# Starting the MLP's first layer early, and replacing in place: one change to a top-k attention and mixer kernel

## The chip, the cores and the metric

The kernel runs on one core of one Trainium2 chip. The time is device microseconds of one execution; the median of seven runs of the kernel before is 1774.5 us (1771.52 to 1776.44).

## The reference

For 8 batches and 8 heads, 576 rows and 64 columns a head. Each row of scores keeps what is not below its 32nd largest value:

```
scores = scale * np.matmul(q, k.transpose(0, 1, 3, 2))
kth = np.partition(scores, -top_k, axis=-1)[..., -top_k:-top_k + 1]      # top_k = 32
scores = np.where(scores >= kth, scores, -1e9)
attn = exp(scores - max) / (sum + 1e-9);  x = attn @ v, heads side by side: (8, 576, 512)
u = x + (x.transpose(0, 2, 1) @ U @ V).transpose(0, 2, 1)                # rank 32
out = u + np.maximum(u @ w_ch1, 0.0) @ w_ch2                            # 512 -> 2048 -> 512
```

q, k and v are float32; U, V and the two weights are float64 and are turned into float32 on the chip.

## The kernel before, in words

**Steps.** A batch has four pairs of heads, a pair five row chunks (four of 128 rows for each of the two heads, and one in which both heads' last 64 rows share the partitions). So there are 8 × 4 × 5 = 160 steps n, with pair g = n // 5 and chunk t = n % 5. A step with t < 4 works on two score chunks of 128 x 576 (one per head), a step with t = 4 on one.

**One step's work.** `scores` multiplies q by k on TensorE into PSUM, and ScalarE copies the result into an Ssb tile (three buffers); it is issued one step ahead. `front` finds the 32nd largest value on VectorE in four rounds of eight: MAX8 gives the eight largest of a chunk (L385, L399), MATCH_REPLACE8 overwrites them with a very small number (L395), and so on. In the kernel before every replacement writes a new rr tile, of which there are three buffers. The two chunks of a step alternate: replacement, replacement, MAX8, MAX8. Then POOL (L402, L403, L421) and ScalarE (L420, L351) mask and exponentiate. `turns` transposes the weights E on TensorE (L474, L479), with ScalarE copying them out (L475, L480) into PT; from step 30 on one of the two heads goes through VectorE and a DRAM tile instead (`blocks`, tiles y and away), over SP's DMA queue. `values` multiplies by v (L508, L512, L498). When a pair is done, `mixed` applies the low-rank mixing and leaves u, transposed, in uT (L533 to L566).

**The MLP.** When a batch's four pairs are done, `mlp(b)` is appended to the list `fillers`. It goes over two parts of the rows (320 and 256 of the 576). In each part the first layer makes 16 hidden tiles hT of 128 x rows: four matmuls (over the four 128-wide slices `cc` of the 512 channels) into one mm tile in PSUM, which has two buffers, and one ReLU on ScalarE (L593). The second layer makes four output tiles from 16 matmuls each (L600); they are copied, u is added on POOL (L616), and a little later they are transposed back and stored by SP's queue.

**Order.** All four compute engines run what the program issues in the program's own order. The MLP's matmuls are spread between the attention's by `fill()`, called eight times a step (four times in the first 20 steps). Each call adds a fixed `share` to a budget `due` and takes matmuls from the first entry of `fillers` until the budget is used up; if there is none, `due` is set to 0. Shares are such that one MLP lasts about as long as the 20 steps of a batch; while n is at most 42 they are 0.91 of that. In the first 20 steps there is no MLP to take from. Steps 19 and 20 have a written-out order of their own, which finishes the first batch quickly.

**Weights.** `params` lists the 36 loads of U, V and slabs of the two weights; `next_params` starts one, and at later calls ScalarE (L174 to L178), VectorE (L186) and POOL (L187, L189) turn it into float32. w1 is complete before the first MLP starts.

Of the kernel before, what the change touches and what calls it, by code (L numbers as in the profile page):

```python
# [8 lines left out]
F32 = mybir.dt.float32  # L9
# [17 lines left out]
def kernel(  # L27
# [28 lines left out]
    nc = tc.nc  # L56
    B, H, S, D = q.shape
    P = 128
    C = H * D
    R = moe_U.shape[1] // 2  # L60
    F = moe_w_ch1.shape[1] // 2
# [15 lines left out]
    HT = 10  # L77
# [121 lines left out]
         [(V[:, at(t)], lambda a, t=t: a.rearrange("r (p t) -> r t p", t=NT)[:, t]) for t in range(NT)]),  # L199
        ([moe_V[:, 2 * MAIN:2 * S]] * NT, [(V[:, at(NT)], same)]),  # L200
    ]
    for f in range(0, F, SLAB):
        for cc in range(NC):
            params.append(
                ([moe_w_ch1[cc * P:(cc + 1) * P, 2 * f:2 * (f + SLAB)]], w1[:, cc, f:f + SLAB])
            )
    for c in range(0, C, P):
        for f in range(0, NF, NT):
            params.append((
# [156 lines left out]
    def front(g, t):  # L366

        if t == 0:
            dens[g] = small.tile([P, 2 * NT + 1], F32, tag="den", name="den", bufs=3)
        chunks, den = S2s.pop((g, t)), dens[g]
        n = len(chunks)
        E2 = attn.tile([P, 2 * S], F32, tag="E", name="E", bufs=3)
        Es = [E2[:, c * S : (c + 1) * S] for c in range(n)]
        sums = [den[:, 2 * t + c : 2 * t + c + 1] for c in range(n)]
        probs[g, t] = E2
        curs, ms = list(chunks), [None] * n
        first = small.tile([P, 2, 8], F32, tag="first", name="first", bufs=3)  # L380
        nmax = small.tile([P, 2], F32, tag="nmax", name="nmax", bufs=4)
        order = (1, 0) if n == 2 else (0,)
        for c in order:
            ms[c] = first[:, c]
            nc.vector.max(ms[c], curs[c])  # L385
        yield
        early, pooled, gaps = ways(g, t)
        for i in range(1, TOPK // 8):
            if i == 1:
                nc.scalar.mul(nmax[:, 0:n], first[:, 0:n, 0], -SCALE)  # L390
                for c in early:
                    weigh(chunks[c], Es[c], nmax[:, c : c + 1])
            for c in order:
                nxt = attn.tile([P, S], F32, tag="rr", name="rr", bufs=3)
                nc.vector.match_replace(nxt, ms[c], curs[c], NEG)  # L395
                curs[c] = nxt
            for c in order:
                ms[c] = small.tile([P, 8], F32, tag="m8", name="m8", bufs=8)
                nc.vector.max(ms[c], curs[c])  # L399
            yield  # L400
        for c in pooled:
            nc.gpsimd.tensor_scalar(Es[c], chunks[c], ms[c][:, 7:8], NEG, ALU.is_lt, ALU.mult)  # L402
            nc.gpsimd.tensor_tensor(chunks[c], chunks[c], Es[c], ALU.add)  # L403
        for c in early:
            nc.vector.scalar_tensor_tensor(
                out=Es[c],
                in0=chunks[c],
                scalar=ms[c][:, 7:8],
                in1=Es[c],
                op0=ALU.is_ge,  # L410
                op1=ALU.mult,
                accum_out=sums[c],
            )
        if t == NT:
            del qkTs[g]
        yield
        for c in gaps:
            least = small.tile([P, 1], F32, tag="least", name="least", bufs=3)
            nc.scalar.mul(least, ms[c][:, 7:8], WIDEN)
            nc.scalar.activation(Es[c], chunks[c], AF.Relu, bias=least, scale=-WIDEN)  # L420
            nc.gpsimd.tensor_tensor(chunks[c], chunks[c], Es[c], ALU.subtract)  # L421
            yield
        ahead = pooled if shared(g, t) else ()
        for c in ahead:
            weigh(chunks[c], Es[c], nmax[:, c : c + 1], sums[c])
            yield
        for c in order:
            if c not in early and c not in ahead:
                weigh(chunks[c], Es[c], nmax[:, c : c + 1], sums[c])
        if t == NT and g != NPAIR - 1:  # L430
            nc.scalar.activation(den, den, AF.Identity, bias=eps)
        yield
# [91 lines left out]
    def mixed(g, wait):  # L524

        b, gi = divmod(g, NPAIR)
        if gi == 0:
            uTs[b] = mlpp.tile([P, NC, S], F32, tag="uT", name="uT")
        XT, den = XTs.pop(g), dens[g]
        X = xs[g % 2]  # L530
        tp = ps_t.tile([P, NT, P], F32, tag="tp", name="tp")
        for t in range(NT):
            nc.tensor.transpose(tp[:, t, :], XT[:, cols(t)], ident)  # L533
        X4 = X[:, 0:NT, :].rearrange("p t (h d) -> p t h d", h=2)
        tp4 = tp.rearrange("p t (h d) -> p t h d", h=2)
        den4 = den[:, 0 : 2 * NT].rearrange("p (t h) -> p t h ()", h=2).to_broadcast([P, NT, 2, D])
        nc.scalar.copy(X4, tp4)
        nc.gpsimd.tensor_tensor(X4, X4, den4, ALU.mult)
        for _ in range(wait):
            yield  # L540
        pT = ps_t.tile([P, P], F32, tag="tp", name="pT")
        for t in range(NT + 1):
            i = t % NT * R
            nc.tensor.matmul(
                pT[i : i + R, :],
                lhsT=U[:, t, :],
                rhs=X[:, t, :],
                start=(t < NT),
                stop=(0 < t),
            )  # L550
        Tb = mlpp.tile([P, P], F32, tag="Tb", name="Tb")
        nc.scalar.copy(Tb, pT)
        yield
        for chunks, (lo, hi) in zip(PARTS, SPAN):
            up = ps_t.tile([P, WIDE], F32, tag="tp", name="up")
            nc.tensor.matmul(up[:, 0 : hi - lo], lhsT=Tb, rhs=V[:, lo:hi], start=True, stop=False)  # L556
            for t in chunks:
                nc.tensor.matmul(  # L558
                    up[:, OFF[t] - lo : OFF[t] - lo + rows(t)],
                    lhsT=X[:, t, :],  # L560
                    rhs=ident if t < NT else ident2,
                    is_transpose=True if t < NT else None,
                    start=False,
                    stop=(t == chunks[-1]),
                )
            nc.scalar.copy(uTs[b][:, gi, lo:hi], up[:, 0 : hi - lo])  # L566
            yield
        if gi == NPAIR - 1:
            fillers.append(mlp(b))

    def mlp(b):

        uT = uTs.pop(b)
        late = []
        for chunks, (lo, hi) in zip(PARTS, SPAN):
            w = hi - lo
            hTs = []
            for f in range(NF):
                ph = ps_m.tile([P, C], F32, tag="mm", name="mm")
                for cc in range(NC):  # L580
                    nc.tensor.matmul(  # L581
                        ph[:, 0:w],
                        lhsT=w1[:, cc, f * P : (f + 1) * P],
                        rhs=uT[:, cc, lo:hi],
                        start=(cc == 0),
                        stop=(cc == NC - 1),
                    )
                    if cc < NC - 1:
                        yield w / C
                if f % 2 == 0:  # L590
                    hT = mlpp.tile([P, 2, WIDE], F32, tag="hT", name="hT", bufs=HT)
                    hTs += [hT[:, 0], hT[:, 1]]
                nc.scalar.activation(hTs[f][:, 0:w], ph[:, 0:w], AF.Relu)  # L593
                if f == 3 and late:
                    late.pop()()
                yield w / C
            for c in range(NC):
                po = ps_m.tile([P, C], F32, tag="mm", name="mm")
                for f in range(NF):
                    nc.tensor.matmul(  # L600
                        po[:, 0:w],
                        lhsT=w2[:, f, c * P : (c + 1) * P],
                        rhs=hTs[f][:, 0:w],
                        start=(f == 0),
                        stop=(f == NF - 1),
                    )
                    if f == 9 and late:
                        late.pop()()
                    if f < NF - 1:
                        yield w / C  # L610
                oT = mlpp.tile([P, WIDE], F32, tag="oT", name="oT")
                if b == B - 1:
                    nc.vector.tensor_tensor(oT[:, 0:w], uT[:, c, lo:hi], po[:, 0:w], ALU.add)  # L613
                else:
                    nc.scalar.copy(oT[:, 0:w], po[:, 0:w])
                    nc.gpsimd.tensor_tensor(oT[:, 0:w], oT[:, 0:w], uT[:, c, lo:hi], ALU.add)  # L616
                late.append(turned_back(b, chunks, lo, c, oT))
                yield w / C
        late.pop()()
# [221 lines left out]
```

## Time and profile before

| | us |
|---|---|
| median of 7 runs | 1774.5 |
| the profiled execution, its own time | 1776.44 |
| its span, first to last instruction | 1774.7 |
| TensorE busy | 1668.6 (94%) |
| VectorE busy | 1561.4 (88%) |
| ScalarE busy | 1029.3 (58%) |
| POOL busy | 846.0 (48%) |
| MAX8, L399: 864 of 749 ns | 614.8 |
| MATCH_REPLACE8, L395: 576 of 742 ns, and 288 of 742 ns in the first round | 427.4 and 211.8 |
| first layer L581, second layer L600 | 542.6 and 547.4 |
| ReLU L593: 256 of 411 ns | 105.2 |

PE is TensorE, PEld its weight loads, DVE is VectorE, ACT ScalarE, SP the engine that issues the DMAs. A float32 matmul stands as two records in the trace. A line of the trace in order of time gives start, length, engine, source line, operation, output and inputs with shapes, how many stand together, and in brackets how long the engine was idle before and what released it. A busy share is an average over stages that have different limits, so the stages are looked at one by one.

### The profile page before, as it was taken

The page shows a single profiled execution, that of the slowest core. Times are in us where ns is not written, and L with a number is a line of the kernel's source. Part 1 is how long each engine was busy: PE and PEld are TensorE (multiplying, and loading weights), DVE is VectorE, ACT ScalarE, POOL GpSimd, SP SyncE. Part 2 cuts the span into 40 slices and gives each one's busy share as a digit, 9 for nine tenths or more (in the row PEclk, how much of TensorE's full clock was granted, in tenths as well). Part 3 has the DMA queues.
Part 4 walks back from the last instruction along what each step waited for, and adds up shares of the span by engine and source line. Part 5 has one row for each costly group of instructions (what it writes and reads, how often), then busy time and mean ns, then how long its engine had stood idle before and what let it go on. Part 6 is the DMA issues. An engine that isn't in the chain of part 4 may idle for free.

```text
span 1774.7 us, 28992 instructions
## 1 busy us (share of the span) xinstructions
PE 1668.6 (94%) x9851; PEld 1256.9 (71%) x9851; DVE 1561.4 (88%) x3106; ACT 1029.3 (58%) x2682; POOL 846.0 (48%) x591
## 2 busy tenths in 40 slices
PE   4566789999999999999999999999999999999999
PEld 2444556677777877788777877788777877788677
DVE  7999999899999999999999999999999999994000
ACT  4778777555656656565656656565656656564100
POOL 4777677535354554545445454444445444453000
PEclk7778899999999999999999999999999999999999
DMA  3222332223233232232233232232233232211010
GB/s 95 87 83 72 88 85 61 50 58 70 58 69 80 63 72 59 64 71 63 63 73 79 62 70 62 64 70 64 63 73 79 60 72 60 53 50 45 4 15 13
DMA packets 275829, 112.79 MB, mean 64 GB/s; under 512 B 173920, under 2 KB 260192, under 8 KB 275680
## 3 DMA queue, kind: packets, MB, share of 16 engines
q1 hardware_dynamic: 274624, 110.68, 26.4%
q8 instruction: 77, 1.26, 0.3%
q14 instruction: 72, 0.59, 0.1%
q10 hardware_dynamic: 1056, 0.26, 0.1%
HBM read 74.15 MB, written 36.70 MB: 62 GB/s over the span
## 4 chain that ended last, share of the span: by engine, by line
PE 76%; DVE 17%; POOL 3%; issue 2%; ACT 1%; DMA 1%; SPq 0%; POOLq 0%; DVEq 0%
PE mm L581 26%; PE mm L600 25%; DVE rr L395 8%; PE sc L333 6%; DVE m L399 6%; PE O L512 6%; PE tp L474 3%; DVE first L385 2%; PE sc L320 2%; PE O L498 2%; PE up L556 1%; PE O L508 1%; POOL E L402 1%; PE tp L648 1%; PE up L558 1%
## 5 line engine op out<-in xcount | busy, mean ns | idle before, releaser
L399 DVE MAX8 m<-rr 128x8 f32<-128x576 f32 x864 | 614.8, 749 | 5.5
L600 PE MATMUL mm<-hT,w 128*128 128x256 f32 (+1 forms) x2048 | 547.4, 410 | 0.0
L581 PE MATMUL mm<-uT,w 128*128 128x256 f32 (+1 forms) x2048 | 542.6, 411 | 3.2 <-ACT hT L593 3.2
L402 POOL TENSOR_SCALAR E<-Ssb,m 128x576 f32<-128x576 f32 x127 | 280.9, 2211 | 414.5 <-DVE m L399 412.8
L581 PEld LDWEIGHTS mm<-uT,w 128*128 128x128 f32 x2048 | 372.1, 191 | 117.5 <-issue 26.2
L600 PEld LDWEIGHTS mm<-hT,w 128*128 128x128 f32 x2048 | 368.3, 190 | 106.8 <-issue 22.5
L395 DVE MATCH_REPLACE8 rr<-m,rr 128x576 f32<-128x576 f32 x576 | 427.4, 742 | 0.0
L421 POOL TENSOR_TENSOR Ssb<-Ssb,E 128x576 f32<-128x576 f32 x159 | 225.0, 1415 | 119.6 <-ACT E L420 119.0
L351 ACT ACTIVATE E<-Ssb,nmax 128x576 f32<-128x576 f32 x288 | 223.2, 776 | 54.3 <-POOL Ssb L403 37.0
L593 ACT ACTIVATE hT<-mm 128x320 f32<-128x320 f32 (+1 forms) x256 | 105.2, 411 | 240.0 <-PE mm L581 239.6
L385 DVE MAX8 first<-Ssb 128x8 f32<-128x576 f32 x288 | 203.4, 743 | 31.5 <-ACT Ssb L346 31.5
L395 DVE MATCH_REPLACE8 rr<-first,Ssb 128x576 f32<-128x576 f32 x288 | 211.8, 742 | 0.0
L403 POOL TENSOR_TENSOR Ssb<-Ssb,E 128x576 f32<-128x576 f32 x127 | 179.1, 1410 | 10.6
L333 PE MATMUL sc<-qkT 64*128 64x288 f32 x1024 | 170.5, 454 | 6.7 <-ACT Ssb L344 5.8
L474 PE MATMUL tp<-ident,E 128*128 128x128 f32 x736 | 116.3, 284 | 36.7 <-ACT XT L521 13.9
L512 PE MATMUL O<-PT,va 128*64 128x128 f32 x2048 | 145.7, 283 | 2.0 <-DMA PT<-away 2.0
L474 PEld LDWEIGHTS tp<-ident,E 128*128 128x128 f32 x736 | 92.3, 146 | 68.6 <-ACT XT L521 15.9
L475 ACT COPY PT<-tp 128x512 f32<-128x512 f32 x184 | 106.8, 586 | 49.7 <-PE tp L474 47.2
L512 PEld LDWEIGHTS O<-PT,va 128*64 128x64 f32 x2048 | 113.5, 139 | 18.8 <-DMA PT<-away 2.7
L420 ACT ACTIVATE E<-Ssb,least 128x576 f32<-128x576 f32 x159 | 123.3, 776 | 5.2
L333 PEld LDWEIGHTS sc<-qkT 64*128 64x128 f32 x1024 | 93.1, 197 | 45.1 <-issue 14.0
L613 DVE TENSOR_TENSOR oT<-uT,mm 128x320 f32<-128x320 f32 (+1 forms) x8 | 3.6, 455 | 137.1 <-PE mm L600 137.1
(81 smaller groups left out, 1573.0 us busy)
## 6 DMA issues: line engine op xcount, KB each, us to landing
away<-y SPq DMA_DIRECT2D x416, 64.0 KB, 1.8
PT<-away SPq DMA_DIRECT2D x104, 256.0 KB, 2.8
raw<-in_moe_w_ch_dram SPq DMA_DIRECT2D x32, 512.0 KB, 3.9
va<-in_v_dram SPq DMA_DIRECT2D x64, 128.0 KB, 2.2
out_dram<-ob SPq DMA_DIRECT2D x57, 128.0 KB, 2.3
ld<-in_q_dram SPq DMA_DIRECT2D x108, 64.0 KB, 2.4
ld<-in_k_dram SPq DMA_DIRECT2D x108, 64.0 KB, 2.4
ld<-in_q_dram SPq DMA_DIRECT2D x108, 8.0 KB, 2.2
```

What stands on the lines that cost most here:

```text
L333: nc.tensor.matmul(sc[:, h, 0:HALF], lhsT=qkT[half(h), 0, cols(t)], rhs=qkT[half(h), 1, i * HALF : (i + 1) * HALF], start=True, stop=True,)
L351: nc.scalar.activation(E, chunk, AF.Exp, bias=nmax, scale=SCALE, accum_out=total)
L385: nc.vector.max(ms[c], curs[c])
L395: nc.vector.match_replace(nxt, ms[c], curs[c], NEG)
L399: nc.vector.max(ms[c], curs[c])
L402: nc.gpsimd.tensor_scalar(Es[c], chunks[c], ms[c][:, 7:8], NEG, ALU.is_lt, ALU.mult)
L403: nc.gpsimd.tensor_tensor(chunks[c], chunks[c], Es[c], ALU.add)
L421: nc.gpsimd.tensor_tensor(chunks[c], chunks[c], Es[c], ALU.subtract)
L474: nc.tensor.transpose(tp[:, j, :], E2[:, a : a + P], ident)
L512: nc.tensor.matmul(O[half(h)], lhsT=va[:, h, j, :], rhs=PB[:, j] if h and shared(g, t) else PT[:, NT * h + j], start=False, stop=(j == NT ...
L581: nc.tensor.matmul(ph[:, 0:w], lhsT=w1[:, cc, f * P : (f + 1) * P], rhs=uT[:, cc, lo:hi], start=(cc == 0), stop=(cc == NC - 1),)
L600: nc.tensor.matmul(po[:, 0:w], lhsT=w2[:, f, c * P : (c + 1) * P], rhs=hTs[f][:, 0:w], start=(f == 0), stop=(f == NF - 1),)
```

## The change

Three things change.

1. The first-layer weights w1 are loaded in another order: the slabs of the channel slices 0 and 1 first (FIRST = 2), for all of the 2048 columns, then those of the slices 2 and 3.
2. When the second pair of the first batch is mixed, a new generator `head_start` is appended to `fillers`. For the first 320 rows of batch 0 it forms, for each of the 16 hidden tiles, the sum over the two channel slices that exist by then (two matmuls), and ScalarE copies that half sum into the hidden tile's place (16 copies, eight hT buffers). When `mlp(0)` later makes these tiles, it brings the half sum back into PSUM by a matmul with the identity and adds only the slices 2 and 3: three matmuls in place of four. The second part of batch 0 and all other batches are as before.
3. In `front`, only the first round's replacement takes a new rr tile; the later rounds write the tile that they read.

```diff
+    FIRST = 2
+    for ccs in (range(FIRST), range(FIRST, NC)):
+        for f in range(0, F, SLAB):
+            for cc in ccs:
+                params.append(
+                    ([moe_w_ch1[cc * P:(cc + 1) * P, 2 * f:2 * (f + SLAB)]], w1[:, cc, f:f + SLAB])
+                )
...
-                nxt = attn.tile([P, S], F32, tag="rr", name="rr", bufs=3)
+                nxt = attn.tile([P, S], F32, tag="rr", name="rr", bufs=3) if i == 1 else curs[c]
                 nc.vector.match_replace(nxt, ms[c], curs[c], NEG)
...
+        if g == FIRST - 1:
+            fillers.append(head_start())
         if gi == NPAIR - 1:
             fillers.append(mlp(b))
+    begun = []
+    def head_start():
+        w = SPAN[0][1]
+        for f in range(NF):
+            ph = ps_m.tile([P, C], F32, tag="mm", name="mm")
+            for cc in range(FIRST):
+                nc.tensor.matmul(
+                    ph[:, 0:w],
+                    lhsT=w1[:, cc, f * P : (f + 1) * P],
+                    rhs=uTs[0][:, cc, 0:w],
+                    start=(cc == 0),
+                    stop=(cc == FIRST - 1),
+                )
+                if cc < FIRST - 1:
+                    yield w / C
+            if f % 2 == 0:
+                hT = mlpp.tile([P, 2, WIDE], F32, tag="hT", name="hT", bufs=HT)
+                begun.extend((hT[:, 0], hT[:, 1]))
+            nc.scalar.copy(begun[f][:, 0:w], ph[:, 0:w])
+            yield w / C
...
-            hTs = []
+            more = b + lo == 0
+            hTs = list(begun) if more else []
             for f in range(NF):
                 ph = ps_m.tile([P, C], F32, tag="mm", name="mm")
-                for cc in range(NC):
+                if more:
+                    nc.tensor.matmul(
+                        ph[:, 0:w], lhsT=ident, rhs=hTs[f][:, 0:w], start=True, stop=False
+                    )
+                    yield w / C
+                for cc in range(FIRST if more else 0, NC):
...
-                        start=(cc == 0),
+                        start=(cc == 0 and not more),
...
-                if f % 2 == 0:
+                if f % 2 == 0 and not more:
```

More of the change, by code (lines that the diff above doesn't have):

```diff
@@ L201 @@
     ]
-    for f in range(0, F, SLAB):
-        for cc in range(NC):
-            params.append(
-                ([moe_w_ch1[cc * P:(cc + 1) * P, 2 * f:2 * (f + SLAB)]], w1[:, cc, f:f + SLAB])
-            )
+    FIRST = 2
[5 more added lines that the diff above has]
+                )
     for c in range(0, C, P):
@@ L576, in mlp @@
             w = hi - lo
-            hTs = []
+            more = b + lo == 0
+            hTs = list(begun) if more else []
             for f in range(NF):
                 ph = ps_m.tile([P, C], F32, tag="mm", name="mm")
-                for cc in range(NC):
+                if more:
[4 more added lines that the diff above has]
+                for cc in range(FIRST if more else 0, NC):
                     nc.tensor.matmul(
```

## The prediction

> **What bounds the kernel now.** I read the page's totals and slices, then stretches of 20 us, then VectorE's, TensorE's and ScalarE's instructions in order of time, then the chain that ended last.
>
> ```profile
> span 1774.7 us, 28992 instructions
> PE 1668.6 (94%) x9851; PEld 1256.9 (71%) x9851; DVE 1561.4 (88%) x3106; ACT 1029.3 (58%) x2682; POOL 846.0 (48%) x591
> ...
> PE   4566789999999999999999999999999999999999
> ...
> DVE  7999999899999999999999999999999999994000
> ...
> PEclk7778899999999999999999999999999999999999
> ...
> PE 76%; DVE 17%; POOL 3%; issue 2%; ACT 1%; DMA 1%; SPq 0%; POOLq 0%; DVEq 0%
> ```
>
> One slice is 44.4 us. VectorE fills the first five or six, TensorE all after the eighth; the chain's 76% and 17% say the same. The stretches (PE, PEld, DVE, ACT, POOL busy) show what is free before the hand-over:
>
> ```profile
> 160.00:180.00 20.00, 8.66 (x53) 5.97 (x53) 19.86 (x42) 15.06 (x34) 15.68 (x12) 0.70 0.31 93
> 180.00:200.00 20.00, 13.18 (x94) 8.68 (x92) 19.69 (x41) 16.55 (x38) 16.42 (x12) 0.78 0.27 70
> 220.00:240.00 20.00, 15.34 (x80) 9.78 (x80) 19.86 (x41) 14.23 (x35) 14.51 (x11) 1.00 0.21 60
> ```
>
> TensorE has 7 to 11 us free in 20, but ScalarE only 3.5 to 5. From 379 us on TensorE is busy without a break but for waits of 0.4 us at 413, 2.06 at 444 and then 0.1 in each batch, so whatever moves the first matmul of the second batch's MLP (449.54 us) moves the end by as much.
>
> VectorE in order of time (a stall, then replacements of round 1 and of round 2):
>
> ```profile
> 261.39 1.42 DVE L385 MAX8 first<-Ssb 128x8 f32<-128x576 f32 x2 [3.98 <-ACT Ssb L346]
> ...
> 262.79 0.74 DVE L395 MATCH_REPLACE8 rr<-first,Ssb 128x576 f32<-128x576 f32 x1
> ...
> 263.52 0.74 DVE L395 MATCH_REPLACE8 rr<-first,Ssb 128x576 f32<-128x576 f32 x1
> ...
> 265.99 0.74 DVE L395 MATCH_REPLACE8 rr<-m,rr 128x576 f32<-128x576 f32 x1
> ...
> 266.84 0.74 DVE L395 MATCH_REPLACE8 rr<-m,rr 128x576 f32<-128x576 f32 x1
> ```
>
> Start to start the pair takes 0.73 us in round 1 and 0.85 in rounds 2 and 3. With three rr buffers the second replacement writes the buffer that the first one still reads, and waits for its end; in round 1 the source is Ssb and there is no such wait.
>
> TensorE at the end of the first batch's MLP:
>
> ```profile
> 444.48 0.56 PE L648 MATMUL tp<-ident,oT 128*128 128x128 f32 x2 [2.06 <-POOL oT L616]
> ...
> 449.54 2.69 PE L581 MATMUL mm<-uT,w 128*128 128x320 f32 x9
> ```
>
> **What the Trainium skill says.** VectorE: DVE Perf Modes, section "The DRAIN you can't avoid", has a semaphore after each of eight copies cost nothing extra. This trace differs: the wait on the instruction just in front costs 0.12 us. The next section, "Two Vector instructions with no wait between them", has an instruction that is not held start before the one in front is done; round 1 agrees (0.73 pitch under 0.74 duration). TensorE: Matmul & The Clock Gate, Part 1, has the array throttled until activity releases it; the granted clock (0.70 and 0.78 above, 1.00 from 200 us) agrees. Perfetto Trace Analysis, "Matmuls", wants groups to rotate through banks so that the emptying of one overlaps the next; here two mm tiles do, and where ScalarE was held up TensorE stood 3.22 us before L581 (239.52 us).
>
> **The change part by part.** *Replacements in place.* Rounds 2 and 3 write their own source, and the second replacement waits only for its maxima. The MAX8 behind them now waits for the first replacement, which has another instruction between: nothing, as in round 1, which has this shape. Saving 2 × 0.12 = 0.24 us in each of the 128 steps with two chunks, 31 us of VectorE in all, but worth time only where VectorE leads: 16 such steps up to step 18 (3.8 us), about two each near 261–282 and 316–337, four in 368–410, two in 418–438. Bounds per step: 0 (the gap is something else) and 0.3.
>
> *Head start.* In the order of the changed program 32 matmuls of 320 columns stand between steps 12 and 21, two of them just ahead of the scores of step 21. One costs 6.63 us / 12 = 0.55 at full clock (at most 0.79, the slowest L581 of this trace). So 17.6 to 25 us of TensorE enter a stage with 31 us free (120 to 200 us), and 16 copies of 128x320 at 0.43 (the uT copy of that size) = 6.9 us enter ScalarE, which has 3.5 to 5 in 20. Cover up to step 18: the score copies end 8 us before VectorE wants them (178.65 against 186.98). At steps 20 and 21 that slack is 1.9 and 2.8 us (203.7 against 205.62, 213.35 against 216.11). ScalarE last waits for VectorE at 165.73 (2.79 us, before L419); the 13 pair steps until then bring that point to 162.6. From there to the same instruction of step 18 (198.27) it has nine copies more, 3.9 us, and some 0.5 us of waits for their matmuls: −3.1 + 3.9 + 0.5 is about 1 us late. The two matmuls ahead of step 21's scores add 1.1 and their copy 0.4, so that the MLP starts 2.5 us later than at 214.16. VectorE's 3.8 us are then used up by waiting; behind it ScalarE's raw passes feed POOL, and scores of steps 23 and 25 follow POOL's sums (the stall shown at 261). I take +2 us at 261; bounds −3.8 (all hidden: quicker matmuls at a released clock, ScalarE's waits swallowing the copies) and +5.
>
> *First layer of part one.* 64 matmuls become 16 with the identity and 32: 16 fewer, −8.8 us. ReLUs come after three matmuls, not four: five more copies (2.2 us) before 262, five fewer after; counted in the +2. The budget `share` per fill stays, so the steps stay as full and the MLP runs out earlier by 16 × 320 columns = 20 matmuls of 256 (8.9 us at 0.44, from L600's 18 records in 3.99 us). From the second MLP's start both orders are the same.
>
> *What moves with it.* The first oT comes a step earlier: POOL's wait of 1.94 us for it at 296.5, which is on the chain, goes, and the ob copies leave ScalarE's queue ahead of the 316 stall (0.5). On SP's queue the out stores no longer stand between the four away stores at 357: 1.1 us. The last oT's wait (2.06) moves into the slack below. The reordered w1 loads keep number and size; of the changed program's 12 needed slabs the last is joined by step 10.
>
> Sum for VectorE's clock: +2 − 0.5 − 1.9 − 0.5 − 0.5 − 1.1 − 1.0 − 0.5 = −4.0 us at 438. Then TensorE, without filler for about 1.4 steps, catches up. How far: L512 of that step needs the PT transfer, fetched at 441.04 and, like the 2.97 us of the one at 360.77, landed at 444; it ran at 446.68, so 2.7 us are to be had, and up to 5 on the steps whose PT is early. I take 2.5; the rest of the 8.9 is idle. Total −6.5 us: 1776.4 becomes 1769.9 in the profiled execution (its span is 1.7 less), 1768.0 on the median of 1774.5. Behind it nothing gives it back: TensorE's step is 10.0 us (200 a batch), VectorE's drops from 9.7 to 9.5.
>
> **The rivals.**
> (a) All hidden: the copies fit into ScalarE's waits, VectorE keeps −3.8 at 261, and the total is −12 us: 1762. For it: TensorE's free 30 us and a clock that more work releases. Against: slacks of 1.9 and 2.8 us, and ScalarE above 80% busy.
> (b) It does only half: the pitch stays 0.85, or TensorE's freed 8.9 us are wholly idle because turns and values wait for E and PT: −2 us, 1772.5, within the noise. For it: VectorE is 97% busy in that stretch. Against: TensorE is 100% busy there, and round 1 has the wait-free shape.
> (c) Slower: ScalarE stands in order behind TensorE's head start at the hand-over. If each of those nine copies waits 1 us for matmuls that stand behind transposes, which wait for ScalarE themselves, and one more stall of two full mm tiles like the 3.22 us at 239 comes with it, 12 us are added: +14 at 261 in place of +2, total +5.5, 1780. It decides once the score copies of steps 20 to 25 are more than 8.5 us later than now. For it: a hand-over with 1.9 us of slack. Against: TensorE's queue there is mostly waiting, so a group is done before ScalarE asks for it.
>
> **How the numbers follow.** My forecast (1764.5 to 1771) 0.47, (a) 0.23, (b) 0.18, (c) 0.12. A measurement of this kernel tells 0.2%, 3.5 us, from no change. Faster: forecast and (a), and a quarter of (b), 0.74; same: the rest of (b) and some of (c), 0.16; slower 0.10. The range 1760 to 1776 leaves out (c) and the far end of (a); the likeliest case alone is 1764.5 to 1771.
>
> **What would show it.** Right: replacement pitch 0.73 in every round; the L581-like matmuls of the head start between 140 and 212 us with granted clock above 0.78; score copies of step 20 a little late; the second MLP's first matmul near 443 instead of 449.5, after a stretch where TensorE idles some 5 us; from there a trace shifted as a whole. Wrong: a pitch still 0.85, VectorE stalls of more than 8 us in 200–262, or TensorE with new breaks after 450.

## The result, and the profile after

The changed kernel takes 1770.5 us (median of 15 runs, 1768.7 to 1772.7) against 1775.5 us (35 runs beside it): a ratio of 0.9974, 95% interval 0.9967 to 0.9981. The gain of 5.0 us, or 4.6 by the ratio, lies within the range and on the side that was forecast; 6.5 us had been forecast. The profiled executions differ by 6.6 us in span (1774.7 and 1768.1).

The page of the changed kernel, its totals, the slices of the granted clock, and the chain:

```profile
span 1768.1 us, 29071 instructions
...
PE 1673.2 (95%) x9883; PEld 1259.3 (71%) x9883; DVE 1539.7 (87%) x3106; ACT 1032.5 (58%) x2698; POOL 846.8 (48%) x591
...
PEclk7788999998999999999999999999999999999999
...
PE 80%; DVE 10%; ACT 4%; POOL 3%; issue 2%; DMA 1%; SPq 0%; POOLq 0%; DVEq 0%
```

VectorE's busy time fell by 21.7 us with the same 3106 instructions of the same mean lengths: they stand closer together and overlap more. Its share of the chain fell from 17% to 10%, and ScalarE's rose from 1% to 4%. In the tenth slice (400 to 444 us) TensorE's clock shows an 8 that the kernel before had not.

Three of the stretches shown of before, and one more at the end of the first batch's MLP (columns: window, length, busy time and records of PE, PEld, DVE, ACT, POOL; then granted clock, DMA share, GB/s):

```profile
160.00:180.00 20.00, 13.95 (x79) 9.62 (x78) 20.00 (x44) 17.25 (x41) 15.90 (x12) 0.83 0.37 119
180.00:200.00 20.00, 17.43 (x109) 11.67 (x108) 19.61 (x41) 16.75 (x42) 13.59 (x11) 0.92 0.25 68
220.00:240.00 20.00, 17.07 (x86) 10.74 (x85) 18.48 (x38) 15.80 (x38) 15.71 (x11) 1.00 0.25 67
420.00:440.00 20.00, 14.56 (x80) 10.75 (x80) 20.00 (x42) 11.91 (x32) 11.68 (x8) 0.81 0.27 63
```

The head start fills TensorE and ScalarE before 200 us, and at 420 to 440 TensorE, which was busy for all of the 20 us before, now idles for 5.4 of them. VectorE there is busy for all of the 20.

VectorE in order of time, the same step as was shown of before:

```profile
260.21 1.42 DVE L388 MAX8 first<-Ssb 128x8 f32<-128x576 f32 x2 [3.98 <-ACT Ssb L349]
...
261.61 0.74 DVE L399 MATCH_REPLACE8 rr<-first,Ssb 128x576 f32<-128x576 f32 x1
...
262.34 0.74 DVE L399 MATCH_REPLACE8 rr<-first,Ssb 128x576 f32<-128x576 f32 x1
...
265.14 0.74 DVE L399 MATCH_REPLACE8 rr<-m,rr 128x576 f32<-128x576 f32 x1
265.80 0.07 DVE L399 MATCH_VALUE_LOAD rr<-m,rr 128x8 f32 x1
265.87 0.74 DVE L399 MATCH_REPLACE8 rr<-m,rr 128x576 f32<-128x576 f32 x1
```

The pair of round 2 now stands 0.73 us apart, as the pair of round 1 does; it was 0.85. Between the two stands a short instruction that loads the values to be looked for (MATCH_VALUE_LOAD). It now starts 0.08 us before the replacement in front ends; before, it started 0.03 us after that end (266.76, behind 265.99 + 0.74). The stall in front of the step is as long as before to the hundredth (3.98).

TensorE in order of time around the start of the second batch's MLP:

```profile
423.81 0.44 PE L684 MATMUL tp<-ident,oT 128*128 128x128 f32 x2 [1.26 <-POOL oT L652]
...
438.54 0.49 PE L512 MATMUL O<-PT,vd 128*128 128x128 f32 x2 [2.00 <-ACT uT L570]
...
440.59 2.26 PE L336 MATMUL sc<-qkT 64*128 64x288 f32 x8
442.78 4.57 PE L617 MATMUL mm<-uT,w 128*128 128x320 f32 x16
```

The second MLP starts at 442.78 instead of 449.54 us: 6.8 us, about as much as the whole result (6.6 by the spans). What follows is nearly the old trace, shifted: the fourth MLP starts 7.9 us early (843.12 instead of 850.97), and the last transfer takes 1.4 us of that back (below).

### The profile page after: what moved, and what is told of

Its sections match the earlier page's. It is cut to its first block, busy times and chain, and to the rows that moved or that the text cites. A ratio compares the mean times of both kernels' runs of the same rounds, so it can differ in the third digit from the quotient of the medians.

```text
span 1768.1 us, 29071 instructions
## 1 busy us (share of the span) xinstructions
PE 1673.2 (95%) x9883; PEld 1259.3 (71%) x9883; DVE 1539.7 (87%) x3106; ACT 1032.5 (58%) x2698; POOL 846.8 (48%) x591
## 4 chain that ended last, share of the span: by engine, by line
PE 80%; DVE 10%; ACT 4%; POOL 3%; issue 2%; DMA 1%; SPq 0%; POOLq 0%; DVEq 0%
PE mm L636 26%; PE mm L617 26%; PE sc L336 7%; PE O L516 6%; DVE rr L399 4%; DVE m L403 4%; PE tp L478 3%; PE O L502 2%; PE sc L323 2%; PE up L560 1%; DVE first L388 1%; PE O L512 1%; PE tp L537 1%; POOL E L406 1%; PE up L562 1%
## 5 line engine op out<-in xcount | busy, mean ns | idle before, releaser
L617 PE MATMUL mm<-uT,w 128*128 128x256 f32 (+1 forms) x1984 | 523.0, 409 | 0.3 <-ACT hT L629 0.3
L617 PEld LDWEIGHTS mm<-uT,w 128*128 128x128 f32 x1984 | 359.6, 190 | 110.0 <-issue 25.2
```

Source lines behind the costliest of these rows:

```text
L617: nc.tensor.matmul(ph[:, 0:w], lhsT=w1[:, cc, f * P : (f + 1) * P], rhs=uT[:, cc, lo:hi], start=(cc == 0 and not more), stop=(cc == NC - 1),)
```

## The experiments

The prediction rested on two separate things: replacements in place make VectorE faster, and the head start costs something at the hand-over and gives it back later through fewer matmuls. The sum came out about right. Whether its terms did, a time of the whole kernel can't tell; each run below does one of them alone.

**The two halves apart.** The kernel before with only the replacement changed:

```diff
-                nxt = attn.tile([P, S], F32, tag="rr", name="rr", bufs=3)
+                nxt = attn.tile([P, S], F32, tag="rr", name="rr", bufs=3) if i == 1 else curs[c]
```

> The kernel before with the replacements in place alone. Theory (both parts are needed: in place makes VectorE early up to step 19, the head start takes the matmuls that would give it back): the pitch of two replacements is 0.73 us in all rounds; VectorE reaches step 19 about 3.6 us early as in the changed kernel; the first MLP starts 2 to 3 us early, since no copies of half sums stand in ScalarE's queue; the second MLP starts 2 to 4 us early, and the time falls by 2 to 4 us (1771.5 to 1773.5). Rival A, all of the gain is the replacements': 4 to 6 us less. Rival B, all of it is the head start's: within 1 us of the kernel before.

And the changed kernel with only that line put back:

```diff
-                nxt = attn.tile([P, S], F32, tag="rr", name="rr", bufs=3) if i == 1 else curs[c]
+                nxt = attn.tile([P, S], F32, tag="rr", name="rr", bufs=3)
```

> The changed kernel with three rr tiles as before, so only the head start and the order of the w1 loads. Theory: pitch 0.85 us; VectorE on the old clock to step 19; the first MLP starts 1.5 to 3.5 us later than before; after it 16 matmuls fewer; the second MLP starts 1 to 3 us early and the time falls by 1 to 3 us (1772.5 to 1774.5). Rival A (all is the replacements'): within 1 us of before, or slower. Rival B (all is the head start's): 4 to 6 us less.

Measured: in place alone 1765.8 us, ratio 0.9949 (0.9935 to 0.9962), 9.5 us less than before; head start alone 1776.9 us, 1.0011 (1.0002 to 1.0019), 1.6 us more. In place alone is better than both kernels, and by more than the theory (2 to 4 us) or rival A (4 to 6) had expected; the head start alone came out as rival A had it. The head start takes 4.7 us from in place alone (1770.5 against 1765.8), by the medians three times what it costs without it.

VectorE in the run with in place alone, the two large stalls in front of steps 25 and 30:

```profile
258.53 1.42 DVE L385 MAX8 first<-Ssb 128x8 f32<-128x576 f32 x2 [3.98 <-ACT Ssb L346]
...
313.04 1.42 DVE L385 MAX8 first<-Ssb 128x8 f32<-128x576 f32 x2 [5.43 <-ACT Ssb L346]
```

Before, the first of them was 3.98 us as well (261.39 us, shown in the prediction), and the second 5.42:

```profile
316.44 1.42 DVE L385 MAX8 first<-Ssb 128x8 f32<-128x576 f32 x2 [5.42 <-ACT Ssb L346]
```

So a step that starts earlier doesn't wait longer for its scores. In the kernel before, the chain behind the stall at 261.39 goes back over ScalarE, POOL and TensorE to maxima of VectorE at 226.12 us, so it moves along with VectorE; only what VectorE gains between those maxima and the stall is swallowed.

The trace of in place alone is 8.93 us early at step 47 and 9.87 at the last one. That looks like 38 steps with two chunks at 0.24 us each (9.1), but it isn't: step by step the gain is uneven. Up to the start of step 19 it is 2.26 us, where 16 steps should give 3.8. In 7 of these 16 (steps 3, 6, 8, 11, 13, 16, 18) L186, VectorE's part of turning the weights into float32, becomes longer by what the replacements save. Step 3 before, and with in place alone:

```profile
46.36 1.10 DVE L186 TENSOR_SCALAR w<-w 128x512 uint32<-128x512 uint32 x1
```

```profile
45.61 1.37 DVE L186 TENSOR_SCALAR w<-w 128x512 uint32<-128x512 uint32 x1
```

Undisturbed it takes 0.41. In all seven steps of both traces it ends 0.28 or 0.29 us after an instruction of POOL ends, so it seems to be held by POOL, which in these steps moves forward by less than VectorE; no run tests this. From step 19 to step 30 another 1.1 us comes, and from step 30 on every step with two chunks pays 0.25 (14 of them up to step 47, 3.5 us). The remaining 2 us are two waits that became shorter: 0.9 at step 35, and 1.0 in step 44 and ahead of step 45.

**Is it the buffer?** In place also saves a buffer and changes what is read. Four buffers in rotation take away the wait and leave the copy as it was (one hT buffer less makes the room):

```diff
-    HT = 10
+    HT = 9
...
-                nxt = attn.tile([P, S], F32, tag="rr", name="rr", bufs=3) if i == 1 else curs[c]
+                nxt = attn.tile([P, S], F32, tag="rr", name="rr", bufs=4)
```

> The changed kernel with four rr tiles in turn in place of replacement in place (and nine hT tiles in place of ten, for the room). If the 0.12 us is the wait for the buffer that the replacement in front still reads, four tiles take it away as well: pitch 0.73, VectorE busy as in the changed kernel, time within 1 us of it. If writing in place is itself what is quicker, the pitch is 0.85 and the time is that of the head start alone.

Measured: 1769.9 us, ratio 0.9971 (0.9960 to 0.9983), as the changed kernel. VectorE's round 2 in step 16 of this run:

```profile
168.50 0.73 DVE L399 MATCH_REPLACE8 rr<-m,rr 128x576 f32<-128x576 f32 x1
...
169.23 0.74 DVE L399 MATCH_REPLACE8 rr<-m,rr 128x576 f32<-128x576 f32 x1
```

and in the run with three buffers and the head start:

```profile
170.31 0.74 DVE L399 MATCH_REPLACE8 rr<-m,rr 128x576 f32<-128x576 f32 x1
...
171.16 0.74 DVE L399 MATCH_REPLACE8 rr<-m,rr 128x576 f32<-128x576 f32 x1
```

0.73 against 0.85 us, and so it is in all 256 pairs of rounds 2 and 3 of each trace (medians 0.727 and 0.854): the gap is the wait for a buffer that the instruction just in front still reads, and nothing else that in place changes.

**The first layer's relief.** 8.9 us of TensorE were to come free, of which 2.5 would move the end. Two runs tried to use the freed time better, by spreading the rest of the first MLP wider:

```diff
-    SLOTS, SHORT, EARLY = 8, 0.65, 0.91
+    SLOTS, SHORT, EARLY = 8, 0.65, 0.85
```

> The changed kernel with the budget per fill in the first 43 steps at 0.85 of a share in place of 0.91, so that the shorter first MLP lasts as long as before and TensorE has no stretch without filler before the second one. Theory (the freed matmuls are partly lost as idle time at a lower granted clock): the granted clock stays at 1.00 between 420 and 440 us, scores come a little earlier in each step, and the time falls by 1 to 3 us against the changed kernel (1767.5 to 1769.5). Rival (that idle time is beside VectorE's clock and costs nothing): within 1 us of the changed kernel.

Measured: 1777.0 us, 1.0013 (1.0005 to 1.0021). This says nothing on the relief. The share also holds for the first steps of the second MLP, which is out of step with the attention from then on. TensorE's waits of this run between 600 and 1600 us (in total, times, longest):

```profile
PE tp L684 <- POOL oT L652: 7.0, 5, 1.4
```

A wait of 1.4 us comes once in each batch (the changed kernel has none there), and between 600 and 800 us TensorE is busy for 198.49 us where it was 199.88. The trace, 9.0 us early at step 48, is 1.1 early at the last step. The run was made again with the smaller share for steps 21 to 40 alone, so that the second MLP keeps its place:

```diff
-            due += share * (SHORT if t == NT else 1) * (EARLY if n <= 2 * ALONE + 2 else 1)
+            due += share * (SHORT if t == NT else 1) * (0.855 if ALONE < n <= 2 * ALONE else EARLY if n <= 2 * ALONE + 2 else 1)
```

> The changed kernel with the budget at 0.855 of a share in steps 21 to 40 alone, so that the first MLP ends just ahead of the second one, whose matmuls then stand in the same places as before to the end. Theory (running dry with the colder clock behind it costs part of what the head start loses): 1 to 3 us less than the changed kernel (1767.5 to 1769.5), still above replacement in place alone. Rival (running dry is free): within 1 us of the changed kernel.

Measured: 1770.9 us, 0.9974 (0.9965 to 0.9983), as the changed kernel and as the rival had it. The test is weak: of the idle time between 400 and 600 us it took only 1.4 us away (TensorE busy 194.57 against 193.20).

The relief alone tells more. In place, no head start, and the first part of the first MLP leaves out channel slice 0: 16 matmuls fewer, and a part of the output is without that slice's share.

```diff
-                for cc in range(NC):
+                skip = 1 if b + lo == 0 else 0
+                for cc in range(skip, NC):
...
-                        start=(cc == 0),
+                        start=(cc == skip),
```

> Replacement in place, no head start, and the first part of the first MLP leaves out channel slice 0 (its output lacks that slice's share): 16 matmuls of 320 columns fewer at the same place as in the change, at no cost ahead. Theory now (between 261 and 450 us VectorE and the chains through POOL and ScalarE set the pace, so the freed matmuls become idle time and a colder clock before the second MLP): between 2 us less and 2 us more than replacement in place alone (1763.8 to 1767.8). Rival (TensorE's work there is on the path, as the prediction's term of -8.8 us has it, half kept): 4 us less or more than that (1762 or below).

Measured: 1767.2 us, 0.9957 (0.9944 to 0.9969), 1.5 us more than in place alone (the intervals overlap), not less, as the theory had it. Its stretch at the end of the first MLP:

```profile
420.00:440.00 20.00, 13.44 (x85) 9.90 (x85) 20.00 (x41) 11.19 (x32) 11.70 (x8) 0.89 0.26 62
```

TensorE has nothing to do for 6.6 us, VectorE is never idle, and the granted clock falls. In sum the freed matmuls buy nothing. That is a sum of two effects. The stall ahead of step 35 is 0.45 or 0.46 us in all six traces in which the first part has 16 matmuls fewer, and 1.2 to 3.8 in the eight others. But the stall ahead of step 25 is 5.25 us here, where it is 3.98 with in place alone.

**What the head start itself costs.** The half sums formed and copied, and then not used (the first MLP runs in full):

```diff
-            more = b + lo == 0
+            more = False
```

> The changed kernel with the half sums formed and copied as in the change but never used: the first MLP computes all four slices, as before. This is the bare cost of the head start beside replacement in place (1765.8 us alone). Theory now (the head start delays the hand-over of steps 19 to 25 by about 2 us, as the steps of the changed kernel against those with replacement in place alone show, and the rest of its cost comes later, from TensorE running dry): 2 to 3 us more than replacement in place alone (1767.5 to 1769). Rival (the whole cost is the head start itself): 4.5 us or more above it (1770 or more).

The same without the head start at all, so with only the new order of the w1 loads and the replacement in place (run twice, the second time beside the last runs):

```diff
-        if g == FIRST - 1:
-            fillers.append(head_start())
...
-            more = b + lo == 0
+            more = False
```

> Replacement in place and the new order of the w1 loads, nothing else. All theories: within 1 us of replacement in place alone (1764.8 to 1766.8), since number, size and times of the loads are the same. If it is 2 us or more above, the order of the loads is part of the cost of the head start.

> e7 once more (in place and the new load order, no head start), so that e9 and e10 have their base on the same chip: 1766.5 within 1 by every theory.

Measured: half sums unused 1770.2 us, 0.9973 (0.9963 to 0.9983); order alone 1766.5, 0.9952 (0.9940 to 0.9965), and again 1766.0, 0.9956 (0.9943 to 0.9968). The order of the loads costs nothing that can be seen. Forming the half sums costs about 4 us, as the rival had it, and in the time of the kernel using them gives back nothing: 1770.2 unused, 1770.5 used. (In the traces the last step starts 1.4 us earlier when they are used, and the last transfer loses 1.3 us again.)

**Matmuls or copies.** The unused half sums, not copied out:

```diff
-            if f % 2 == 0:
-                hT = mlpp.tile([P, 2, WIDE], F32, tag="hT", name="hT", bufs=HT)
-                begun.extend((hT[:, 0], hT[:, 1]))
-            nc.scalar.copy(begun[f][:, 0:w], ph[:, 0:w])
             yield w / C
```

> As e5 (all 32 matmuls of the half sums, not used afterwards), but nothing copies them out: the 16 copies of 128x320 on ScalarE are left out. Theory S (ScalarE's copies, 6.9 us in a queue above 80% busy, are what the hand-over pays for): as e7, 1766.5 within 1. Theory M (the matmuls do it, by standing ahead of transposes and scores on TensorE): as e5, 1770.2 within 1. In between: both.

Measured: 1766.7 us, 0.9962 (0.9949 to 0.9974), within 0.7 us of the order alone. The 32 matmuls are hidden, as said; the 16 copies on ScalarE are what costs. (With the copies the run also leaves out the eight hT buffers that they fill; the two weren't taken apart.) The traces show one place. ScalarE in the changed kernel, between the steps 18 and 20:

```profile
194.70 0.41 ACT L598 COPY hT<-mm 128x320 f32<-128x320 f32 x1
...
197.41 0.41 ACT L598 COPY hT<-mm 128x320 f32<-128x320 f32 x1
...
198.38 0.41 ACT L598 COPY hT<-mm 128x320 f32<-128x320 f32 x1
...
201.49 1.44 ACT L354 ACTIVATE E<-Ssb,nmax 128x576 f32<-128x576 f32 x2
```

VectorE in the same kernel:

```profile
203.06 0.17 DVE L490 TENSOR_SCALAR den<-den 128x8 f32<-128x8 f32 x1 [1.92 <-ACT E L354]
...
204.18 1.42 DVE L388 MAX8 first<-Ssb 128x8 f32<-128x576 f32 x2
215.09 1.42 DVE L388 MAX8 first<-Ssb 128x8 f32<-128x576 f32 x2 [0.58 <-ACT Ssb L349]
```

And without the copies, ScalarE and then VectorE:

```profile
199.93 1.44 ACT L354 ACTIVATE E<-Ssb,nmax 128x576 f32<-128x576 f32 x2
```

```profile
202.38 0.15 DVE L490 TENSOR_SCALAR den<-den 128x8 f32<-128x8 f32 x1
...
203.38 1.41 DVE L388 MAX8 first<-Ssb 128x8 f32<-128x576 f32 x2
```

Step 19 has a written-out order in which VectorE, after its maxima, waits for ScalarE's exponentials of that step. With the copies these come 1.6 us later, and VectorE stands for 1.92 us where it did not stand at all. It had come 1.2 us earlier than without the copies (its L186 of step 18 took 0.50 us in place of 1.40), so step 20 starts 0.8 us later. The stall ahead of step 23 adds another 1.1: 1.52 us in place of 0.41. At step 25 the changed kernel is 1.7 to 2.9 us later than the four traces with in place and without the copies (in place alone, both of the order alone, and this one).

It is tempting to say that in place uses up a cover that the head start lived on: in the kernel before, ScalarE was through at 202.60 us and VectorE came at 204.62. The trace of the head start alone doesn't bear this out. There VectorE stands at the same place for 1.49 us, and against before step 20 starts 0.8 us late and step 24 1.7. With in place the same steps are 0.8 and 2.2 later than without the copies. Only at step 25 do the two part, 0.9 against 2.3, and there the kernel before is the odd one: its L186 in step 24 took 1.55 us, in the other three traces 0.8 to 0.9. Why the head start costs 1.6 us in one case and over 4 in the other stays open.

**Only where it meets the hand-over?** Half sums for eight of the 16 tiles, unused, the last of which is copied at 173 us, before step 17:

```diff
-        for f in range(NF):
+        for f in range(NF // 2):
```

> In place, new load order, half sums formed for only 8 of the 16 hidden tiles (16 matmuls, 8 copies) and, as in e5, not used afterwards. They end about four steps before the hand-over (step 20). Theory H (the head start costs what it does only where it meets the hand-over, steps 18 to 21): as e7, 1766.5 within 1, the shift of step 25 within 0.6 us of e7's. Theory T (it costs by the amount of work put in, wherever it stands): half of e5's 3.7, so 1768.3.

> e9 once more, for a second trace of it. e9's trace is level with e11's at step 25 (0.03 us earlier) and at step 34 (0.10 earlier), as theory H has it, yet its time is 3.3 us above e11's; the trace shows 1.5 us of that at step 35, where the PT tile fetched from DRAM landed later, and 1.15 behind the last step. If these belong to the kernel they come again: step 25 within 0.3 us of e11's, the stall of step 35 near 3.2, step 159 to the end near 163.7, time 1769. If they were chance: the stall below 2, the end 162.6 and time 1766.5, and H stands in full. If step 25 is now 1 us or more late, H falls.

Measured: 1769.3 us, 0.9972 (0.9963 to 0.9982), and again 1769.4, 0.9967 (0.9955 to 0.9979). The hand-over is free, as the first theory had it: against the order alone, step 25 starts 0.03 us earlier, in the second trace 1.59 earlier. Yet some 3 us are lost all the same (the executions that were profiled lose 2.4 and 2.6 of them). TensorE at steps 34 to 35 and in the last step, eight tiles:

```profile
359.48 1.34 PE L516 MATMUL O<-PT,va 128*64 128x128 f32 x14 [2.66 <-DMA PT<-away]
...
1616.88 1.09 PE L516 MATMUL O<-PT,va 128*64 128x128 f32 x14 [0.72 <-DMA PT<-away]
```

and the order alone, which has no wait for a fetch in its last step:

```profile
358.71 1.09 PE L516 MATMUL O<-PT,va 128*64 128x128 f32 x14 [1.80 <-DMA PT<-away]
```

In both traces of the eight tiles the last step loses time: its start is followed by 163.7 and 164.0 us, against 162.5 in both traces of the order alone, because the last fetch of the tile PT from DRAM lands late. The stall ahead of step 35 tells nothing: it is 3.23 and 3.81 us here, but 1.75 and 3.08 in the two traces of the order alone. So the last fetch accounts for 1.2 to 1.4 us, and for the rest no place was found that both traces share.

The theory that the cost sits at the hand-over alone falls: none of the 15 executions with eight tiles is below 1768.3 us, and none of the 10 of the order alone above 1767.6. The theory that it goes with the amount is missed by 1 us (1768.3 had been said), which the intervals don't exclude. Why eight copies that ended at 173 us should delay the end, and the last fetch at 1613, none of the runs tells; this stays open. The changed kernel pays at the end as well: it waits 0.97 us for its last fetch and has 163.9 us behind the last step's start; before, there was no such wait, and 162.3.

One caution comes with it: the two traces of the order alone differ by up to 0.7 us in where a step beyond step 20 starts, and by 1.3 in the stall of step 35; those of the eight tiles by 1.6 at step 25. Shifts of single steps below that are not evidence, here as in the parts above; the medians carry the verdicts.

## Why the prediction was right, and where its steps were not

The total was right by luck: four of its terms were wrong by 2 to 3 us each, and the errors cancelled (the hand-over, POOL's wait, the way to step 35, and TensorE's catching up). By the prediction's own terms, in place was worth −3.8 at the hand-over and −0.5, −0.5, −1.0, −0.5 after it, together −6.3 us. The head start was the rest: +5.8 at the hand-over, −1.9, −0.5, −1.1 and −2.5 after it, together −0.2. Measured are −9.5 and +4.7. Step by step, in us against the kernel before (a step starts with its first MAX8; the changed kernel is 0.3 us ahead from its first step on):

| | forecast | changed kernel | in place alone |
|---|---|---|---|
| start of step 25 (261 us) | +2.0 | −1.2 | −2.9 |
| start of step 30 (316 us) | −0.9 | −1.4 | −3.4 |
| start of step 35 (369 us) | −2.5 | −5.1 | −5.3 |
| start of step 42 (440 us) | −4.0 | −6.4 | −6.9 |
| first matmul of the second MLP | −6.5 | −6.8 | −8.4 |
| end of the span | −6.5 | −6.5 | −9.6 |

- *The wait for the buffer, 0.12 us a pair.* Right, and shown by four buffers. The pitch and the mechanism were as said.
- *"Worth time only where VectorE leads", 26 steps.* Failed in size, on both sides. Up to step 18 the 16 steps were worth 2.3 us with in place alone, not 3.8, because L186 took the gain back in seven of them. Behind it they were worth more: the stall ends a chain that starts at VectorE's own maxima, so it keeps its length and moves, and from step 30 to step 47 all 14 steps pay, where 8 had been counted from 316 us on. Together with the two waits that became shorter this makes the term 3.2 us too small.
- *The copies on ScalarE at the hand-over.* The mechanism was right: score copies and exponentials come late behind the copies, while the matmuls are free. The size was too much. Counted from step 18 to step 25, the changed kernel loses 2.1 to 3.0 us to the four traces without the copies, not 5.8. At 261 us it stood 1.2 us earlier than before, where +2 had been said. But the eight tiles lose some 3 us with no delay at the hand-over, so the prediction's picture of the cost isn't the whole of it.
- *POOL's wait of 1.9 us at 296 and the 0.5 at the 316 stall.* Failed. From step 25 to step 30 it took 55.05 us before, 54.87 after and 54.54 with the order alone, and the stall at step 30 is 5.43. The wait is still there, before the same sum of POOL:

```profile
295.13 0.87 POOL L652 TENSOR_TENSOR oT<-oT,uT 128x320 f32<-128x320 f32 x1 [1.96 <-ACT oT L651]
```

- *The out stores that no longer stand between the away stores, 1.1 us.* The gain came, and was larger: step 35's stall is 0.46 us after and 3.18 before. In the same program without the head start it was 1.75 and 3.08, so 1.3 to 2.6 us. That the out stores are the reason wasn't tested; what the runs show is that it comes with the 16 matmuls fewer.
- *"TensorE catches up", 2.5 us of the freed 8.9.* Failed. TensorE's second MLP starts 6.8 us early where VectorE's step 42 was 6.4 early: 0.4 us, not 2.5. Without the head start the freed matmuls bring nothing either. In 420 to 440 us VectorE is busy for 20.00 us of 20. The idle stretch of "some 5 us" is there (5.4), and behind it the clock is low: 0.81, and the scores at 440.59 take 2.26 us, where the same eight records at 418.95 took 1.24. With four buffers TensorE idles there for as long (5.8 us, clock 0.83), but the slow records fall on other matmuls; the scores take 1.24 and the second MLP starts at 441.26. The slow scores thus cost the changed kernel about 1 us at this place. That the end comes later for it isn't shown: the two programs take the same time (1770.5 and 1769.9).
- *"Behind it nothing gives it back."* Nearly: the shift against before is −7.3 us at step 47 and −8.2 at the last step, but 1.7 of it is gone at the end of the span, with the last fetch.
- *The second MLP's first matmul near 443, head start at a clock above 0.78.* Right: 442.78, and 0.83 and 0.92 in the two stretches.

Of the readings of the lines, one was off: the free time of "7 to 11 us in 20" holds for the two stretches up to 200 us; in 220 to 240 TensorE had 4.7, and ScalarE 5.8 in place of "3.5 to 5".

Of the rivals, (a), all hidden, did not come: the matmuls hide, the copies don't. (b) had the relief right, "wholly idle", and the pitch wrong. (c) asked for score copies late by over 8.5 us; at step 20 the last one came at 203.88 us, 0.4 later than before (203.45) and 1.6 later than in the run without copies (202.31).

## What to carry to other kernels

Where the work that ends a stall of the leading engine starts from that engine itself, the stall moves along when the engine becomes faster, and swallows only what is gained within the chain: follow the chain back before giving the steps around it no value. A saving can also be taken back on the same engine: here an instruction that ends with another engine's work grew by what the replacements saved. Work that is put into idle time has to be priced on each engine that it touches: 32 matmuls were free, and with 16 small copies on an in-order queue they cost 4 us, of which only a part was found in the traces. And two changes that meet at one place aren't added: by the medians the head start costs more with in place than without, so the better kernel is the one with in place alone (1765.8 us). A forecast that comes true in the sum says little about its terms; runs that do one part alone tell them apart.

## What was not expected of the hardware

- The wait on the instruction just in front costs 0.12 us of VectorE on an operation of 0.74 us; without it this kernel takes 9.5 us less. The Trainium skill (VectorE: DVE Perf Modes, "The DRAIN you can't avoid") has a semaphore after each of eight copies cost nothing; for replacements that write what the instruction in front still reads, the run with four buffers shows that it does.
- A weight conversion on VectorE (L186, 0.41 us undisturbed) took up to 1.4 us and ended 0.28 or 0.29 us after an instruction of POOL in all of 14 cases. It so took back 0.25 us in each of seven steps.
- Early work on TensorE goes with a higher granted clock. From 120 to 200 us TensorE was busy for 60.8 to 62.9 us at a granted clock of 0.83 to 0.87 in the seven traces with the whole head start, and for 48.6 to 54.1 at 0.71 to 0.82 in the five without any. Two traces of one program (the order alone) show 0.73 and 0.82, so a single trace tells little. Taking work away does the reverse (0.81 and 0.89 in the idle stretches above, 1.00 with the order alone). That the clock follows activity is as the skill's page TensorE: Matmul & The Clock Gate, Part 1, has it.
- The last fetch of 256 KB from DRAM took 4.1 us from issue to landing in the changed kernel, 3.8 and 4.1 in the two traces with eight tiles, 3.2 to 3.4 in three others with the head start, and 2.6 to 2.8 in the remaining eight, among them before, in place alone, the order alone (twice) and the half sums unused. It is the same transfer in all of them. Two programs were traced twice, and each gave nearly its first value again; the cause wasn't found.
